# A new line of work with five-step weight decoding, queries first among the loads, and zero products behind the first scores

## The chip, the core and the metric

The kernel runs on one core of a Trainium2 chip. The core has five engines that run side by side, each through its own instructions in the order in which they stand in its queue: TensorE (PE in the profile; PEld is its weight loads), VectorE (DVE), ScalarE (ACT), GpSimd (POOL) and SyncE (SP), which here only issues loads. They meet through semaphores. The metric is the device time of one execution in microseconds (us), the median of three runs.

## The reference

Eight batches with eight heads each. 512 local queries attend to the 32 global keys and to local keys no more than 32 positions away; 32 global queries attend to all 544 keys. The result, 544 rows of 512 per batch, goes through a gated layer with a causal convolution of five taps:

```python
s_ll = np.where(np.abs(pos[:, None] - pos[None, :]) <= 32, scale * q_l @ k_l.T, -1e9)
out_l = softmax([scale * q_l @ k_g.T, s_ll]) @ [v_g, v_l]
out_g = softmax(scale * q_g @ [k_g, k_l].T) @ [v_g, v_l]
x = heads side by side of [out_g, out_l]                # (8, 544, 512)
gate = sigmoid(sum(conv_w[k] * xp[:, k:k + S] for k in range(5)))
out = (gate * (x @ w_val)) @ w_out
```

The weights and taps reach the kernel as float64 (it sees them as pairs of 32-bit words); q, k and v are float32.

## The kernel before

The work is cut into 32 units: unit u holds two heads of batch u // 4, so four units make a batch. The steps of a unit have short names, which stand in one long string, `ORDER`. That string is the order in which everything is issued; a planner outside the kernel wrote it. What follows `:` names the engine, what follows `@` the PSUM banks.

- `s` (PE, line 522): scores of a unit, 64 small products; `mx.0`, `mx.1` (DVE, 233): mask added, row minimum taken, four instructions each; `exp` (ACT, 541); `t` (PE, 555): transposes; `tc` (ACT or DVE, 331): copy out of PSUM to `pts`; `av` (PE, 574): times the values; `eps`, `norm` (DVE): division, into `xs`; `xt` (PE, 601): transposes; `xc` (ACT or DVE): copy to SBUF; `xh`, `xl`: high and low part of it for the projections.
- `gs`, `gmax`, `gexp`, `gt`, `gtc`, `gav`, `geps`, `gnorm`, `gx`, `gxc`: the same for the global queries of a batch.
- `tap`, `conv` (DVE): convolution of a unit; for the units 0 and 1 TensorE does it with diagonal matrices instead (`pc`, 678; the diagonals are `dg`, on GpSimd). `sig` (ACT): the sigmoid.
- `g1` (PE, 706) projects by w_val, `gv`, `gh`, `gl` multiply by the gate and split in high and low, `g2` (PE, 734) projects by w_out, `ob` copies the output tile, `st` stores it. Key `g` (`g1.g`, `ob.g.0`, `st.g.1`) is the same for the global rows of all batches, which come last.
- `w0` to `w7`: the decoding of eight 128x512 slices of w_val (0 to 3) and w_out (4 to 7) from float64 words to a high and a low float32 part. `w.s0` takes the magnitude (ACT or DVE), `w.s1` to `w.s7` are seven DVE instructions, `w.high` copies the high part. `cw` does the same for the taps.
- `z` (PE, 805): products of zeros, which compute nothing that is used. `zr` holds zeros as float32r, `zf` as float32.

Loads are issued by SP. The first thirteen stand in `FIRST` (w: a slice of w_val, 512 KB; m: mask and taps, 148 KB; q: queries and keys of a unit, 624 KB; v: its values, 975 KB); each later one is tied to the product before it in the line. An engine that reaches an instruction whose operand has not come waits there, and all that is queued behind it waits too.

`RINGS` gives the number of buffers for each kind of tile. The diff touches `f64_parts` (283), `taps` (312), `weight` (356), the strings, and the loop that makes the `z` steps. The last step that copies an output tile, `ob.g.1`, is split in two: ACT takes the left half, DVE the right.

## Time and profile before

| | |
|---|---|
| median of 3 runs | 350.95 us (350.72 to 354.19) |
| profiled execution, its own time | 352.35 us |
| its span | 350.6 us |
| busy: PE, DVE, ACT, POOL | 334.6, 309.0, 225.1, 13.6 us |

The span runs from the first to the last instruction; 1.75 us lie around it in the profiled execution. Busy time is the sum of the instructions of an engine. A row of the timeline gives start, length, engine, line and operation, a count where alike instructions are merged, and in brackets how long the engine had stood idle before it and which engine's work ended that.

### The profile page before, as it was taken

How to read it: one execution, taken by the hardware profiler on the slowest of the kernel's cores; microseconds unless marked ns; L12 is line 12 of the kernel's file. 1: busy time of each engine (PE TensorE's matmuls, PEld its weight loads, DVE VectorE, ACT ScalarE, POOL GpSimd, SP SyncE). 2: the span in 40 equal slices, each digit the busy share in tenths (PEclk: the TensorE clock that was granted, in tenths of full speed). 3: DMA queues.
4: the chain of work that ended last, by engine and by line, in shares of the span. 5: the costliest groups of instructions: out<-in, count | busy, mean ns of one | idle time of the engine just before them, and what ended most of it. 6: DMA issues, size and time to landing. Idle time of an engine off the chain costs nothing.

```text
span 350.6 us, 15343 instructions
## 1 busy us (share of the span) xinstructions
PE 334.6 (95%) x6658; PEld 268.9 (77%) x6658; DVE 309.0 (88%) x1035; ACT 225.1 (64%) x579; POOL 13.6 (4%) x23
## 2 busy tenths in 40 slices
PE   4889999999999989999999999999999999999994
PEld 1647678778777878887888888787888888888893
DVE  3799999999999989999999999799598898997981
ACT  2678799977878858948947459637876504434221
POOL 4013120001000000000000000000000000000000
PEclk9999999999999999999999999999999999999999
DMA  7987696798477937806393549346460200012124
GB/s 238 410 355 235 214 395 223 226 326 305 170 258 241 344 123 279 285 16 208 116 383 119 179 149 306 145 145 223 146 261 5 80 14 30 2 60 90 65 87 150
DMA packets 17107, 66.64 MB, mean 190 GB/s; under 512 B 1808, under 2 KB 3984, under 8 KB 17040
## 3 DMA queue, kind: packets, MB, share of 16 engines
q1 hardware_dynamic: 12240, 57.01, 46.1%
q10 hardware_dynamic: 4800, 8.65, 6.6%
q8 instruction: 52, 0.85, 0.9%
q14 instruction: 15, 0.12, 0.1%
HBM read 56.74 MB, written 8.91 MB: 187 GB/s over the span
## 4 chain that ended last, share of the span: by engine, by line
PE 86%; DMA 4%; DVE 4%; ACT 3%; issue 2%; ACTq 0%; SPq 0%
PE psum L706 27%; PE psum L734 25%; PE psum L522 9%; PE psum L574 8%; PE psum L263 6%; PE psum L477 3%; PE psum L601 2%; DMA v<-in_vw_dram 2%; PE psum L425 2%; DMA qk<-in_qk_dram 2%; PE psum L555 1%; DVE pm L233 1%; PE psum L678 1%; DVE wa L233 1%; ACT pm L541 1%
## 5 line engine op out<-in xcount | busy, mean ns | idle before, releaser
L233 DVE SCALAR_TENSOR_TENSOR gate<-xc,cw,gate 128x512 f32<-128x512 f32 x120 | 87.7, 751 | 1.0
L541 ACT ACTIVATE pm<-pm,mx 128x128 f32<-128x128 f32 x256 | 80.1, 394 | 10.6 <-DVE mx L233 10.6
L233 DVE CUSTOM_DVE_ANT_0 pm<-psum,small 128x128 f32<-128x128 f32 x256 | 57.8, 286 | 11.1 <-PE psum L522 11.1
L706 PE MATMUL psum<-xh,wvh 128*128 128x512 f32 x128 | 52.0, 407 | 0.0
L734 PE MATMUL psum<-woh,gh 128*128 128x512 f32 x128 | 51.7, 404 | 0.0
L706 PE MATMUL psum<-xh,wvl 128*128 128x512 f32 x128 | 50.1, 391 | 0.9 <-issue 0.9
L734 PE MATMUL psum<-wol,gh 128*128 128x512 f32 x128 | 50.0, 391 | 0.1
L734 PE MATMUL psum<-woh,gl 128*128 128x512 f32 x128 | 50.0, 391 | 0.0
L706 PE MATMUL psum<-xl,wvh 128*128 128x512 f32 x128 | 49.9, 390 | 0.0
L522 PE MATMUL psum<-qk 64*32 64x128 f32 x2048 | 37.0, 282 | 3.5 <-DMA qk<-in_qk_dram 3.3
L690 ACT ACTIVATE gate<-gate 128x512 f32<-128x512 f32 x32 | 19.8, 629 | 29.6 <-DVE gate L233 29.6
L522 PEld LDWEIGHTS psum<-qk 64*32 64x32 f32 x2048 | 30.1, 108 | 9.0 <-DMA qk<-in_qk_dram 4.9
L574 PE MATMUL psum<-v,pts 128*32 128x65 f32 x2048 | 34.4, 221 | 2.1 <-issue 1.9
L574 PEld LDWEIGHTS psum<-v,pts 128*32 128x32 f32 x2048 | 30.5, 109 | 7.4 <-issue 3.0
L331 ACT COPY pts<-psum 128x512 f32<-128x512 f32 x53 | 29.6, 586 | 5.3 <-DVE mx L233 2.8
L706 PEld LDWEIGHTS psum<-xh,wvl 128*128 128x128 f32 x128 | 24.0, 188 | 6.5 <-issue 1.3
L706 PEld LDWEIGHTS psum<-xh,wvh 128*128 128x128 f32 x128 | 24.0, 188 | 6.0 <-DVE gv L233 0.3
L734 PEld LDWEIGHTS psum<-woh,gh 128*128 128x128 f32 x128 | 24.4, 190 | 5.0 <-DVE gm L233 0.2
L734 PEld LDWEIGHTS psum<-woh,gl 128*128 128x128 f32 x128 | 24.0, 188 | 5.2
L734 PEld LDWEIGHTS psum<-wol,gh 128*128 128x128 f32 x128 | 24.1, 188 | 5.0 <-issue 0.5
L706 PEld LDWEIGHTS psum<-xl,wvh 128*128 128x128 f32 x128 | 24.1, 188 | 4.6 <-issue 0.2
L233 DVE SCALAR_TENSOR_TENSOR gv<-gate,psum 128x512 f32<-128x512 f32 x32 | 21.8, 683 | 5.9 <-PE psum L706 3.9
(124 smaller groups left out, 517.2 us busy)
## 6 DMA issues: line engine op xcount, KB each, us to landing
v<-in_vw_dram SPq DMA_DIRECT2D x32, 975.0 KB, 6.9
qk<-in_qk_dram SPq DMA_DIRECT2D x32, 624.0 KB, 5.3
out_dram<-ob ACTq DMA_DIRECT2D x32, 256.0 KB, 2.3
wraw<-in_w_val_dram SPq DMA_DIRECT2D x4, 512.0 KB, 12.5
wraw<-in_w_out_dram SPq DMA_DIRECT2D x4, 512.0 KB, 3.5
out_dram<-obg SPq DMA_DIRECT2D x4, 64.0 KB, 1.7
out_dram<-obg ACTq DMA_DIRECT2D x4, 64.0 KB, 2.0
small<-in_mask_dram SPq DMA_DIRECT2D x1, 148.0 KB, 3.3
```

The lines of the kernel that those rows point to most:

```text
L233: ins = made(*args, **kwargs)
L263: on_pe(T.matmul(out, in_, ident[D * r:D * r + D, D * r:D * r + D], is_transpose=True, **more))
L331: A.copy(out, in_)
L425: on_pe(T.matmul(s[h][SG * c:SG * c + SG, cols], qkt[rows, SL + SG * h:SL + SG * h + SG], keys, start=True, stop=True))
L477: on_pe(T.matmul(ag[SG * c:SG * c + SG, :], pgt[:k, s, SG * c:SG * c + SG], vt[:k, w, h, :], start=(n == 0), stop=(n == len(steps) - 1)))
L522: on_pe(T.matmul((sx, sy)[h][32 * j:32 * j + 32, i, :], qkt[rows, 32 * m:32 * m + 32], qkt[rows, k0:k0 + P], start=True, stop=True))
L541: A.activation(out=pm[:, h, i, :], in_=pm[:, h, i, :], func=AF.Exp, bias=mx[:, c:c + 1], scale=-1.0)
L574: on_pe(T.matmul(ax[32 * j:32 * j + 32, h, E1 * i:E1 * i + E1], q, vt[:, block_win(4 * i + j), h, :], start=True, stop=True))
L601: on_pe(T.matmul(xt[:, P * i:P * i + P], xs[:, i].rearrange("p h d -> p (h d)"), ident, start=(i == 0 or u not in XP), stop=(u not in XP), ...
L690: A.activation(out=g, in_=g, func=AF.Tanh, scale=0.5)
L706: on_pe(T.matmul(box["pv", e], w[:, e, t * P:t * P + P], x, start=(t == 0 and q == 0), stop=(t == NDT - 1 and q == 2)))
L734: on_pe(T.matmul(box["po", r], g[:, e, rs], w[:, e, :], start=(e == 0 and q == 0), stop=(e == NDT - 1 and q == 2)))
```

## The change

1. The decoding loses two of its DVE steps for each slice. Before, the low word's part was made as a float in several steps. Now the mantissa's next bits are cut out of the low word with a shift and put into the float32 word with an or (`s4`), and the low part is the difference between that float and the high part (`s5`). `w.high` now waits for `s4`, so the high part is rounded from the whole float. `cw` loses one small step.
2. `FIRST`: the first unit's queries come first, then w0 and the mask; q3 moves ahead of v0; w2 moves behind v1 and v2.
3. The line is written anew, from the first step to the last. The steps `z1.1` and `z2.0` (three float32r products of zeros) become `z2.0f` (two float32 products of zeros, behind `s0`) and one `z1.1`; `xn0` and `xn3` (a subtraction on TensorE) go, and `xl0` and `xl3` are done on DVE.
4. `RINGS`: more buffers for mx, xg, xs, ob, fewer for xc, xl, gate, xh.

```diff
-FIRST = "w0 m0 q0 q1 q2 v0 w1 w2 q3 v1 w3 v2 v3"
-RINGS = {"mx": 8, ..., "xg": 2, ..., "xc": 7, "xs": 3, ..., "xl": 6, "gate": 7, "xh": 6, "gv": 3, "ob": 6}
+FIRST = "q0 w0 m0 q1 q2 q3 v0 w1 v1 v2 w2 w3 v3"
+RINGS = {"mx": 13, ..., "xg": 5, ..., "xc": 6, "xs": 4, ..., "xl": 5, "gate": 6, "xh": 5, "gv": 3, "ob": 8}
...
-w0.s0:ACT cw dg0 w0.s1 w0.s2 s0@31 mx0.0 exp0.0 s1@50 t0.0@3 tc0.0:ACT mx0.1 mx1.0 mx1.1 exp0.1 t0.1@0 s2@43 exp1.1
+w0.s0:ACT s0@10 mx0.0 exp0.0 w0.s1 z2.0f@7 t0.0@4 mx0.1 s1@21 exp0.1 t0.1@3 tc0.0:DVE cw tc0.1:ACT gs0@35 dg0 mx1.0 s2@20
...
-    def f64_parts(raw, a, low, on=lambda n: "DVE"):
+    def f64_words(raw, a, on="DVE"):
...
-        kept = 0x3FFFFFF8 if low is None else 0x3FFFF000
...
-        power = lambda: V.tensor_scalar(out=hi, in0=a, scalar1=-0x00800000, scalar2=None, op0=ALU.bitwise_and)
-        scaled = lambda x, out: V.scalar_tensor_tensor(out=out, in0=x, scalar=2.0 ** -52, in1=hf, op0=ALU.mult,
-                                                       op1=ALU.mult)
-        if low is None:
-            return first + (power, lambda: scaled(lo.bitcast(U32), lf))
-        return first + (lambda: V.tensor_scalar(out=hi, in0=hi, scalar1=0x1FF, scalar2=None, op0=ALU.bitwise_and),
-                        lambda: V.scalar_tensor_tensor(out=lf, in0=hi, scalar=2.0 ** 32, in1=lo.bitcast(U32),
-                                                       op0=ALU.mult, op1=ALU.add),
-                        power, lambda: scaled(lf, low))
+        return (magnitude,
+                lambda: V.tensor_scalar(out=af, in0=af, scalar1=2.0 ** -15, scalar2=None, op0=ALU.max),
+                lambda: V.tensor_scalar(out=a, in0=a, scalar1=3, scalar2=0x3FFFFFF8, op0=ALU.logical_shift_left,
+                                        op1=ALU.bitwise_and),
+                lambda: V.scalar_tensor_tensor(out=a, in0=hi, scalar=-0x40000000, in1=a, op0=ALU.bitwise_and,
+                                               op1=ALU.bitwise_or),
+                lambda: V.scalar_tensor_tensor(out=a.bitcast(U32), in0=lo.bitcast(U32), scalar=29, in1=a.bitcast(U32),
+                                               op0=ALU.logical_shift_right, op1=ALU.bitwise_or))
...
+        def rest():
+            V.tensor_tensor(out=lo_t, in0=box["a"].bitcast(F32), in1=hi_t.bitcast(F32), op=ALU.subtract)
...
-        plan.add(f"w{k}.high", ("ACT", "DVE", "POOL"), high, [f"w{k}.s3"], lock=True)
+        plan.add(f"w{k}.high", ("ACT", "DVE", "POOL"), high, [f"w{k}.s4"], lock=True)
+        plan.add(f"w{k}.s5", "DVE", rest, [f"w{k}.high"], lock=True)
...
-            plan.add(name, "PE", lambda name=name: keep_clock(int(name[1:].split(".")[0]), HOME[name][0]))
+            plan.add(name, "PE", lambda name=name: keep_clock(int(name[1:].split(".")[0]), HOME[name][0], zf if name[-1] == "f" else zr))
```

The opening on SP, before (q is `qk`, w1 and w3 load into the second half of `wraw0` and `wraw2`):

```order
L349 DMA wraw0_87<-in_w_val_dram 128x4x256
L959 DMA small_71<-in_mask_dram 128x296
L349 DMA qk0_90<-in_qk_dram 128x1248
L349 DMA qk1_92<-in_qk_dram 128x1248
L349 DMA qk2_94<-in_qk_dram 128x1248
L349 DMA v0_96<-in_vw_dram 128x1950
L349 DMA wraw0_87<-in_w_val_dram 128x4x256
L349 DMA wraw2_99<-in_w_val_dram 128x4x256
L349 DMA qk3_101<-in_qk_dram 128x1248
L349 DMA v1_103<-in_vw_dram 128x1950
L349 DMA wraw2_99<-in_w_val_dram 128x4x256
L349 DMA v2_106<-in_vw_dram 128x1950
```

and now:

```order
L337 DMA qk0_87<-in_qk_dram 128x1248
L337 DMA wraw0_89<-in_w_val_dram 128x4x256
L951 DMA small_71<-in_mask_dram 128x296
L337 DMA qk1_92<-in_qk_dram 128x1248
L337 DMA qk2_94<-in_qk_dram 128x1248
L337 DMA qk3_96<-in_qk_dram 128x1248
L337 DMA v0_98<-in_vw_dram 128x1950
L337 DMA wraw0_89<-in_w_val_dram 128x4x256
L337 DMA v1_101<-in_vw_dram 128x1950
L337 DMA v2_103<-in_vw_dram 128x1950
L337 DMA wraw2_105<-in_w_val_dram 128x4x256 x2
L337 DMA v3_108<-in_vw_dram 128x1950
```

q0 comes first, q3 moves ahead of v0, and the pair w2, w3 stands behind v2 instead of around q3 and v1.

The opening on PE, before (qk0 with 32x128 is `s0`, pm0 is `t0`, v0 is `av0`, xs0 is `xt0`, qk0 with 32x384 begins `gs0`):

```order
L805 MATMUL psum_70<-zf_82 128x512 x2
L522 MATMUL psum_70<-qk0_90 32x128 x32
L522 MATMUL psum_70<-qk1_92 32x128 x32
L555 MATMUL psum_70<-ident_72,pm0_173 128x128 x8
L522 MATMUL psum_70<-qk2_94 32x128 x32
L574 MATMUL psum_70<-v0_96,pts0_175 32x65 x32
L555 MATMUL psum_70<-ident_72,pm1_216 128x128 x8
L601 MATMUL psum_70<-ident_72,xs0_335 128x128 x4
L805 MATMUL psum_70<-zr_81 128x512
L425 MATMUL psum_70<-qk0_90 32x384
```

and now:

```order
L797 MATMUL psum_70<-zf_82 128x512 x2
L514 MATMUL psum_70<-qk0_87 32x128 x32
L797 MATMUL psum_70<-zf_82 128x512 x2
L547 MATMUL psum_70<-ident_72,pm0_156 128x128 x4
L514 MATMUL psum_70<-qk1_92 32x128 x32
L547 MATMUL psum_70<-ident_72,pm0_156 128x128 x4
L417 MATMUL psum_70<-qk0_87 32x384
...
L514 MATMUL psum_70<-qk2_94 32x128 x32
L547 MATMUL psum_70<-ident_72,pm1_210 128x128 x4
L566 MATMUL psum_70<-v0_98,pts0_158 32x65 x32
L547 MATMUL psum_70<-ident_72,pm1_210 128x128 x4
L593 MATMUL psum_70<-ident_72,xs0_367 128x128 x4
```

Two float32 products of zeros stand between `s0` and `t0.0`, `s1` goes behind `t0.0`, and `gs0` moves ahead of `s2`.

ACT from `exp1.0` (before) on, around the decoding of w2 (`wa2<-wraw2`), before:

```order
L541 ACTIVATE pm1_216<-pm1_216,mx1_217 128x128 x4
L291 ACTIVATE wa1_331<-wraw0_87 128x512
L291 ACTIVATE wa2_352<-wraw2_99 128x512
L331 COPY xc0_356<-psum_70 128x512
L541 ACTIVATE pm2_276<-pm2_276,mx2_277 128x128 x4
L331 COPY pts1_218<-psum_70 128x512
L331 CAST xh0_390<-xc0_356 128x512
L331 COPY pts1_218<-psum_70 128x512
L291 ACTIVATE wa3_396<-wraw2_99 128x512
L438 ACTIVATE pg0_0_388<-pg0_0_388,gm0_0_387 128x544
L541 ACTIVATE pm2_276<-pm2_276,mx2_277 128x128 x4
L541 ACTIVATE pm3_432<-pm3_432,mx3_433 128x128 x8
```

and now, from `exp2.1` on:

```order
L533 ACTIVATE pm2_290<-pm2_290,mx2_291 128x128 x4
L288 ACTIVATE wa1_363<-wraw0_89 128x512
L430 ACTIVATE pg0_0_313<-pg0_0_313,gm0_0_312 128x544
L319 COPY pts1_212<-psum_70 128x512
L319 COPY pts2_292<-psum_70 128x512
L456 COPY pgt0_0_440<-psum_70 96x384
L457 COPY pgt0_0_440<-psum_70 128x256
L288 ACTIVATE wa2_443<-wraw2_105 128x512
L533 ACTIVATE pm2_290<-pm2_290,mx2_291 128x128 x4
L533 ACTIVATE pm3_428<-pm3_428,mx3_429 128x128 x4
L430 ACTIVATE pg0_1_446<-pg0_1_446,gm0_1_445 128x544
L533 ACTIVATE pm3_428<-pm3_428,mx3_429 128x128 x4
```

`w2.s0` still stands ahead of the first half of `exp2`, but its load now comes later, and `exp2.0`, `exp3.0`, `gexp0.1` and `exp3.1` are queued behind it.

The last rows of DVE, before (obg_1 is the right half of `ob.g.1`, ob7_2 is `ob.7.2`):

```order
L233 SCALAR_TENSOR_TENSOR gvg_2_6165<-gateg2_6001,psum_70 128x256
L233 TENSOR_TENSOR glg_6137<-gvg_2_6165,ghg_6136 128x256
L233 SCALAR_TENSOR_TENSOR gvg_3_6175<-gateg3_6004,psum_70 128x256
L233 TENSOR_TENSOR glg_6137<-gvg_3_6175,ghg_6136 128x256
L233 TENSOR_SCALAR ob7_2_6201<-psum_70 128x512
L233 TENSOR_SCALAR obg_1_6206<-psum_70 128x256
```

and now:

```order
L231 SCALAR_TENSOR_TENSOR gvg_2_6150<-gateg2_5994,psum_70 128x256
L231 SCALAR_TENSOR_TENSOR gvg_3_6152<-gateg3_5997,psum_70 128x256
L231 TENSOR_TENSOR glg_6138<-gvg_2_6150,ghg_6137 128x256
L231 TENSOR_TENSOR glg_6138<-gvg_3_6152,ghg_6137 128x256
L231 TENSOR_SCALAR obg_1_6187<-psum_70 128x256
L231 TENSOR_SCALAR obg_0_6194<-psum_70 128x512
```

The last output tile but one, `ob.g.0`, was ACT's; it is now DVE's, in one piece, behind the half of `ob.g.1`.

## Rows read from the trace of the kernel before

**Rows 1.** Page, busy us (share of the span) xinstructions of each engine.

```profile
PE 334.6 (95%) x6658; PEld 268.9 (77%) x6658; DVE 309.0 (88%) x1035; ACT 225.1 (64%) x579; POOL 13.6 (4%) x23
```

**Rows 2.** Busy time by stretch: PE, PEld, DVE, ACT, POOL (x), PEclk, DMA share, GB/s.

```profile
30.00:40.00 10.00, 9.69 (x271) 6.80 (x270) 9.91 (x35) 9.97 (x25) 4.33 (x5) 1.00 0.69 240
40.00:60.00 20.00, 19.18 (x502) 14.93 (x492) 19.32 (x83) 16.90 (x49) 1.75 (x2) 1.00 0.82 295
60.00:250.00 190.00, 187.18 (x4467) 152.65 (x4466) 178.37 (x639) 139.14 (x369) 1.74 (x2) 1.00 0.63 218
250.00:340.00 90.00, 90.00 (x947) 75.64 (x946) 77.63 (x173) 39.30 (x89) 0.00 (x0) 1.00 0.18 68
```

**Rows 3.** Instructions in order of time, PE: start, us, line, operation [idle before].

```profile
1.43 3.78 PE L805 MATMUL psum<-zf 128*128 128x512 f32 x4 [1.43 <-DVE zero L233]
8.52 3.67 PE L522 MATMUL psum<-qk 64*32 64x128 f32 x128 [3.30 <-DMA qk<-in_qk_dram]
12.12 1.00 PE L555 MATMUL psum<-ident,pm 128*128 128x128 f32 x4
15.22 1.16 PE L522 MATMUL psum<-qk 64*32 64x128 f32 x64
35.31 2.81 PE L678 MATMUL psum<-xc,diag 128*128 128x512 f32 x6
```

**Rows 4.** The same, DVE.

```profile
4.59 0.18 DVE L233 TENSOR_SCALAR cva<-small 128x20 int32<-128x20 int32 x1 [2.64 <-DMA small<-in_mask_dram]
10.58 0.29 DVE L233 CUSTOM_DVE_ANT_0 pm<-psum,small 128x128 f32<-128x128 f32 x1 [3.69 <-PE psum L522]
13.98 0.69 DVE L233 SCALAR_TENSOR_TENSOR wa<-wraw,wa 128x512 int32<-128x512 int32 x1
52.06 0.29 DVE L233 CUSTOM_DVE_ANT_0 pm<-psum,small 128x128 f32<-128x128 f32 x1
```

**Rows 5.** The same, ACT.

```profile
10.92 1.28 ACT L541 ACTIVATE pm<-pm,mx 128x128 f32<-128x128 f32 x4 [6.08 <-DVE mx L233]
```

**Rows 6.** The same, SP, which issues the loads.

```profile
11.26 0.43 SPq L349 DMA_DIRECT2D wraw<-in_w_val_dram  x1
11.74 2.06 SPq L349 DMA_DIRECT2D v<-in_vw_dram  x2
```

**Rows 7.** DMA issues of these stretches: KB each, median us from issue to landing.

```profile
wraw<-in_w_val_dram SPq DMA_DIRECT2D x1, 512.0 KB, 12.0
v<-in_vw_dram SPq DMA_DIRECT2D x1, 975.0 KB, 13.8
```

**Rows 8.** Groups of instructions, DVE: xcount | busy us, mean ns | idle before.

```profile
L233 DVE TENSOR_SCALAR wa<-wa 128x512 f32<-128x512 f32 (+1 forms) x16 | 6.9, 434 | 0.1
L233 DVE SCALAR_TENSOR_TENSOR wa<-wraw,wa 128x512 int32<-128x512 int32 x8 | 5.5, 688 | 0.1
L233 DVE SCALAR_TENSOR_TENSOR wraw<-wraw 128x512 f32<-128x512 int32 x8 | 5.6, 705 | 0.1
L233 DVE SCALAR_TENSOR_TENSOR wvl<-wraw 128x512 fp32r<-128x512 f32 x4 | 2.9, 723 | 0.0
L233 DVE TENSOR_TENSOR xl<-xc,xh 128x512 fp32r<-128x512 f32 x30 | 20.5, 685 | 0.1
L233 DVE COPY pts<-psum 128x512 f32<-128x512 f32 x11 | 7.4, 686 | 0.4 <-PE psum L263 0.4
L233 DVE CAST xh<-xc 128x512 fp32r<-128x512 f32 x9 | 3.8, 421 | 0.0
```

**Rows 9.** Instructions in order of time at the end: PE, ACT, DVE, ACT's queue.

```profile
345.64 0.39 PE L734 MATMUL psum<-woh,glg 128*128 128x512 f32 x1
346.44 0.38 ACT L740 ACTIVATE obg<-psum 128x256 f32<-128x256 f32 x1 [0.49 <-PE psum L734]
346.86 0.42 DVE L233 TENSOR_SCALAR obg<-psum 128x256 f32<-128x256 f32 x1 [4.08 <-ACT obg L740]
347.31 0.86 ACTq L946 DMA_DIRECT2D out_dram<-obg  x2
```

## The prediction

> **What bounds the kernel now.** I first read the page's busy shares: TensorE is busy for 334.6 of 350.6 us, DVE for 309.0 [rows 1]. Then the busy time by stretch: TensorE works for 187.18 of 190 us between 60 and 250, and for 90.00 of 90 from 250 to 340, while DVE and ACT still have room there. Between 30 and 60, DVE (9.91 of 10, 19.32 of 20) and, at first, ACT (9.97) are as full as TensorE [rows 2]. So behind 60 us the time is TensorE's work, which this change leaves nearly alone. What can be won is TensorE's lost time ahead of it, and there the timeline of DVE is the one to follow. Its first row minimum starts at 10.58, after 3.69 us of waiting for the first scores; these start at 8.52, after 3.30 us of waiting for a load [rows 3, 4]. From then on DVE hardly rests: 16 minimum instructions take 10.58 to 13.98, 0.85 us for a half unit, and the seventh unit's begin at 52.06 [rows 4]. I count how much earlier DVE has done the same work in the new line, and take TensorE to be as much ahead when it becomes the bound.

> **The change part by part.**

> (a) The first minimum needs the scores of unit 0 and the mask. The first zeros keep TensorE until 5.21 and the queries now come first: the 660 KB of w0 and mask, ahead of the queries before, had landed by 4.59 [rows 4], and q0 is 624 KB. The scores of two units took 3.67 us [rows 3], so `s0` ends near 7.2 with its latency. The mask now stands last of the 1,284 KB that had landed at 8.52: at the latest it comes then, at the earliest at 6.2 (4.5, and 624 KB at the rate worked out under (e)). I take 7.4: **-3.2 us** (ends -4.0 and -2.1).

> (b) Two float32 products of zeros now stand ahead of `t0.0` on TensorE. The same two took 3.78 us at the start; products of that shape take 2.81 / 3 = 0.94 each at 35 us. The scores show the same two speeds: 3.67 / 2 = 1.84 us for a unit at 8.52, 1.16 at 15.22 [rows 3]. [...] The new zeros then end between 7.2 + 1.9 = 9.1 and 7.2 + 3.8 = 11.0. `t0.0` also needs `exp0.0`, whose four activations start 0.34 us behind the first minimum and take 1.28 [rows 5]: 7.4 + 1.6 = 9.0, so the zeros decide. Its four transposes took 1.00 at 12.12 [rows 3], half of that at the higher clock. For `t0.0` waits DVE, which now does `tc0.0` ahead of the taps and of unit 1. It is there at 7.4 + 0.85 + 0.43 + 0.85 = 9.5, and the copy costs 0.69 [rows 8]. I take zeros that end at 9.9 and transposes of 0.5, a wait of 0.9: **+1.6 us**. [...]

> [...]

> (c) The decoding. Before, a slice took seven DVE steps: four on one tensor (434 ns; `s1` and `s2` have the row, and I price `s4` and `s6`, of the same shape, by it), `s3` with 688, `s5` with 705, `s7` with 685 to 723: 4 x 0.434 + 0.688 + 0.705 + 0.70 = 3.83 us. Now it takes 2 x 0.434 + 2 x 0.688 + 0.685 = 2.93, with `s5` priced as the same difference in `xl` [rows 8]. The new `s4`, a shift with an or on two tensors, has no row; its bounds are 0.434 and 0.723, and I take the 688 of `s3`, which also works on two tensors of integers. That saves 0.90 for a slice, and six slices (w0 to w5) are worked off by 52 us: **-5.4 us**.

> (d) What DVE takes over from ACT and TensorE by then: `xl0` and `xl3` (0.685 each), `xc0` out of PSUM (0.69), `xh0`, `w0.high` and `w3.s0` (0.42 each, by the row of xh), `gxc0` and `geps0` (under 0.42 together): **+3.6 us** [rows 8]. It saves ACT about as much, which is full only between 30 and 40.

> (e) w2 lands later. The loads had brought 1,284 KB at 8.5 and 6,642 KB at 11.26 + 12.0 = 23.3 [rows 3, 6, 7]: 362 KB per us. w2 now stands at 7,105 KB, so at 24.6 (v2, at 7,617 KB, had landed at 25.5). ACT's `w2.s0` follows in about 0.7, until 25.3. DVE gets to `w2.s1` at 24.0: from 7.4 on it has the minima of three units (5.1), (b), nine decoding steps (5.2), the taps (six of 0.18 as at 4.59 [rows 4]), `xc0`, `xh0`, `w0.high` (1.5), and `gmax` twice and `norm0`, priced as three copies of 0.69. That would be a wait of 1.3. But q0's 624 KB took 4.0 us behind the mask, where 1.7 would do at that rate; if this pause goes with the new order, w2 is in time. The middle: **+0.6 us** (ends 0 and the second rival).

> (f) The end. DVE now copies `ob.g.0` behind its half of `ob.g.1`, which itself waited for ACT's half: 346.44 to 346.82 on ACT, 346.86 to 347.28 on DVE. The two stores that ACT issues behind it take 0.86 us [rows 9]. Now the copy (0.69, by the row of pts [rows 8]) comes next, and two more stores stand behind those two: **+0.85 us**, at the least +0.4 if the queue takes them faster.

> Removed products: `xn0`, `xn3` and two float32r zeros go from TensorE, each under the 0.94 of a float32 product [rows 3]; the work that hides this is DVE's, which TensorE waits for at that time, so I count nothing (end -2). Gaps of TensorE between 60 and 250 are 190 - 187.18 = 2.82 us [rows 2]. The new order with its shorter rings makes its own; I take the same amount, with -1 and +2.8 as ends.

> Sum: -3.2 + 1.6 - 5.4 + 3.6 + 0.6 + 0.85 = -1.95 us. The profiled execution took 352.35, 1.4 over the median, so it would take 350.4; the median, 350.95, becomes **349.0 us**, -0.6%.

> **The rivals.** About 1% (3.5 us) is what a measurement of this kernel can tell from no change.

> *The opening works in full* (chance 0.27): mask early (-4.0), zeros short (+0.8), w2 in time (0), the rest as above: -4.15, **346.8 us**. For it: the pause of 2.3 us in the loads under (e). Against it: nothing in the rows says that the new order is rid of that pause.

> *w2 holds up ACT* (0.10), the case on the slower side. If w2 lands no sooner than v3, the last load, at 25.5 + 975 / 362 = 28.2, then ACT stands until 28.9 with four exponential steps queued behind, and DVE waits 4.9 us instead of 0.6: -1.95 + 4.3 = +2.35, **353.3 us**. The time is slower than before from a landing at 25.9 on. For it: slices of 512 KB land late here, 12.0 us behind their issue. Against it: v3 is issued behind w2.

> *The opening's gain is spent in the middle* (0.13): xc, xl, xh and gate each lose a buffer, and TensorE's gaps of 2.82 us double: **351.8 us**. For it: every step stands in a new place. Against it: the old line, written in the same way, left only 2.82 us in 190.

> *The zeros do not do what they are there for* (0.08): the clock stays at 1.2 GHz, (b) is +3.2: **350.6 us**.

> **The numbers.** The forecast has 0.42, and is the likeliest. Its own ends are 347.5 and 350.3. Taking in the first rival, the unknown gaps on its side, and the second rival, 8 times in 10 the time lies between 346.0 and 352.4. Faster by over 1% (under 347.4) is the first rival and a sliver of the forecast: 0.28. Slower by over 1% (over 354.5) needs two of the slower cases together: 0.06. The rest, 0.66, is within 1%.

> **What would show it.** Right: the scores start at about 5.2, the first minimum at 7.2 to 8.5; DVE waits for TensorE ahead of `tc0.0` for up to 1 us and for `w2.s0` near 25; the seventh unit's minimum starts between 45 and 48, with `conv3.0` and the second batch's `gmax` still to come; a slice has five DVE steps of 2.9 us; and 4.5 + 0.85 us lie between the last product and the end. Wrong: a first minimum at 8.5 or later (mask), zeros that end at 11 (b), a wait of DVE or ACT for w2 of more than 2 us (e), over 4 us of gaps in TensorE from 60 to 250, or an end no longer than before (f).

## The result

| | before | changed |
|---|---|---|
| median, first set of runs | 351.88 us | 353.45 us |
| ratio to the kernel before, 95% interval | | 1.0065 (1.0040 to 1.0089) |
| the same kernel once more, another set (`e12_again`) | 352.33 us | 353.25 us, 1.0030 (1.0000 to 1.0061) |
| profiled execution: time, span | 352.35, 350.6 us | 354.58, 352.8 us |
| start of TensorE's last product | 345.64 us | 347.03 us |
| from that product's end to the span's end | 4.57 us | 5.38 us |

The forecast was 349.0 us with a range up to 352.4. By the two sets the change makes the kernel 0.65% and 0.3% slower, the latter with an interval that begins at no change at all: still within the 1% that I called no change, but on the other side, and outside the range. The ratios and their intervals come from the single runs; they need not equal the quotient of the two medians (1.0045 and 1.0026).

### The profile page after: what moved, and what is told of

It is laid out like the page before. It is cut to its first block, busy times and chain, and to the rows that moved or that the text cites. A ratio compares the mean times of both kernels' runs of the same rounds, so it can differ in the third digit from the quotient of the medians.

```text
span 352.8 us, 15328 instructions
## 1 busy us (share of the span) xinstructions
PE 335.9 (95%) x6663; PEld 268.5 (76%) x6663; DVE 309.0 (88%) x1024; ACT 222.7 (63%) x573; POOL 12.9 (4%) x23
## 4 chain that ended last, share of the span: by engine, by line
PE 87%; DVE 3%; DMA 2%; issue 2%; ACT 2%; POOL 1%; DVEq 0%; ACTq 0%
PE psum L726 27%; PE psum L698 25%; PE psum L514 8%; PE psum L566 8%; PE psum L261 6%; PE psum L417 2%; PE psum L469 2%; DMA v<-in_vw_dram 2%; PE psum L670 2%; PE psum L593 2%; PE psum L797 2%; PE psum L547 1%; POOL diag L231 1%; DVE wa L231 1%; ACT pm L533 1%
## 5 line engine op out<-in xcount | busy, mean ns | idle before, releaser
L319 ACT COPY pts<-psum 128x512 f32<-128x512 f32 x49 | 27.8, 587 | 14.1 <-PE psum L261 8.6
L514 PEld LDWEIGHTS psum<-qk 64*32 64x32 f32 x2048 | 29.3, 105 | 7.6 <-issue 4.1
```

The source lines that it names most:

```text
L319: A.copy(out, in_)
L514: on_pe(T.matmul((sx, sy)[h][32 * j:32 * j + 32, i, :], qkt[rows, 32 * m:32 * m + 32], qkt[rows, k0:k0 + P], start=True, stop=True))
```

## The profile after

The page's line of busy time [rows 1] hardly moves: DVE is at 309.0 again, since what the decoding saves goes into copies and splits that ACT or TensorE did before.

```profile
PE 335.9 (95%) x6663; PEld 268.5 (76%) x6663; DVE 309.0 (88%) x1024; ACT 222.7 (63%) x573; POOL 12.9 (4%) x23
```

Busy time by stretch, in the columns of [rows 2], with the first 30 us in front:

```profile
0.00:17.00 17.00, 13.13 (x308) 7.68 (x308) 9.63 (x60) 7.29 (x19) 4.83 (x13) 1.00 0.91 349
17.00:30.00 13.00, 12.03 (x180) 6.56 (x168) 11.74 (x44) 10.48 (x30) 1.18 (x2) 1.00 0.92 335
30.00:40.00 10.00, 7.92 (x238) 5.46 (x239) 8.84 (x34) 7.29 (x19) 4.10 (x5) 1.00 0.67 212
40.00:60.00 20.00, 18.44 (x418) 13.65 (x420) 18.44 (x79) 15.80 (x42) 1.23 (x2) 1.00 0.77 266
60.00:250.00 190.00, 187.00 (x4556) 153.37 (x4557) 175.80 (x630) 137.26 (x366) 1.53 (x2) 1.00 0.63 214
250.00:340.00 90.00, 90.00 (x950) 75.61 (x949) 81.29 (x175) 42.01 (x95) 0.00 (x0) 1.00 0.19 71
```

The kernel before, same stretches:

```profile
0.00:17.00 17.00, 10.94 (x232) 6.93 (x236) 8.88 (x52) 7.28 (x19) 4.75 (x13) 1.00 0.88 321
17.00:30.00 13.00, 11.60 (x246) 7.26 (x235) 12.65 (x54) 10.14 (x28) 1.01 (x1) 1.00 0.80 308
```

Add TensorE's busy time up to 60 us: 13.13 + 12.03 + 7.92 + 18.44 = 51.52 us, of which 1.98 are the new zeros. Before it was 10.94 + 11.60 + 9.69 + 19.18 = 51.41. **In this execution TensorE has, by 60 us, where it becomes the bound, done no more work than before.** It wins in the first 30 us and gives it back between 30 and 60. Busy time is a rough count of work (before, the first two units' scores took 3.67 us of it, now 2.32), and this execution is the latest of six that share this opening: it reaches record 2,500 of TensorE's stream (counted as below) at 62.27 us, the five others (`e12_again`, `e2_idle_load`, `e3_tail`, `e5_late_load`, `e15_two_loads`) at 59.97 to 61.08, with 52.7 to 53.6 us of busy time by 60. Of the kernel before there is one profiled execution.

TensorE in order of time (answers to [rows 3]; last column: idle before, and what ended it):

```profile
5.03 1.16 PE L514 MATMUL psum<-qk 64*32 64x128 f32 x64
6.12 1.98 PE L797 MATMUL psum<-zf 128*128 128x512 f32 x4
8.82 1.16 PE L514 MATMUL psum<-qk 64*32 64x128 f32 x64
12.44 0.86 PE L514 MATMUL psum<-qk 64*32 64x128 f32 x41
15.05 0.51 PE L514 MATMUL psum<-qk 64*32 64x128 f32 x17 [1.76 <-issue]
37.23 0.33 PE L491 MATMUL psum<-ident,xg 128*128 128x128 f32 x1 [1.57 <-DVE xg L231]
57.88 0.50 PE L698 MATMUL psum<-xl,wvh 128*128 128x512 f32 x1 [1.33 <-issue]
117.12 0.76 PE L469 MATMUL psum<-v,pgt 96*32 96x65 f32 x34 [1.39 <-DMA v<-in_vw_dram]
165.76 0.34 PE L261 MATMUL psum<-ident,pm 64*128 64x64 f32 x4 [0.46 <-issue]
190.13 0.32 PE L566 MATMUL psum<-v,pts 128*32 128x65 f32 x8 [0.79 <-issue]
```

DVE (answers to [rows 4]):

```profile
6.89 0.29 DVE L231 CUSTOM_DVE_ANT_0 pm<-psum,small 128x128 f32<-128x128 f32 x1 [4.95 <-DMA small<-in_mask_dram]
8.93 0.69 DVE L231 COPY pts<-psum 128x512 f32<-128x512 f32 x1
15.61 0.29 DVE L231 CUSTOM_DVE_ANT_0 pm<-psum,small 128x128 f32<-128x128 f32 x1 [1.30 <-PE psum L514]
34.13 0.69 DVE L231 TENSOR_TENSOR wvl<-wa,wvh 128x512 fp32r<-128x512 f32 x1 [1.06 <-POOL wvh L231]
47.82 0.32 DVE L231 CUSTOM_DVE_ANT_0 pm<-psum,small 128x128 f32<-128x128 f32 x1
```

The opening starts better than forecast: first minimum at 6.89 (before 10.58), no wait ahead of `tc0.0` at 8.93, seventh unit's minimum at 47.82 (before 52.06). But TensorE stops for 1.76 us in the midst of `s2`, between two products with the same operands at hand, and DVE's next minimum, unit 2's, waits 1.30 us for it. The "issue" idle is the profile's word for a wait for nothing that it shows. The second loss is at 34.13: DVE's `w1.s5` needs `w1.high`, which POOL does behind five diagonals (`dg1`), and behind DVE stands `gnorm0`, for which TensorE waits until 37.23.

What "issue" is can be counted out. I numbered TensorE's records in the trace (weight loads, products, and the 50 of its sequencer) from the first on, and put beside them when the DMA queue that the page calls "instruction" started a packet. It has 52 packets of 16 KB. The stream has 13,376 records, with 52 borders if one stands every 256 records from 193 on (the last is 13,249).

```profile
q8 instruction: 52, 0.85, 1.0%
```

```
                number of the record behind the stall; (its rest modulo 256); stall, us
before          1473 (193) 0.82   3009 (193) 0.88   5825 (193) 1.03
changed          449 (193) 1.76   2241 (193) 1.33   7873 (193) 0.46   8897 (193) 0.79
changed, again   449 (193) 1.36   2241 (193) 0.52   4033 (193) 0.36   4801 (193) 1.25   5825 (193) 0.63   8897 (193) 0.51
```

Every one stands at the border of a block of 256 records, and the packet for that block started 2.3 to 2.9 us before TensorE went on (12.62 for 15.05, 55.56 for 57.88). So TensorE's instructions come by DMA, a block at a time, and TensorE stalls where it is through with one before the next has come. That loads on the DMA engines hold the blocks up is what the experiments test.

## Experiments

All are timed against the kernel before; the changed kernel stands at 1.0065 and 1.0030. The stalls (TensorE's "issue" idle of over 0.15 us) are those of the one profiled execution.

**Where the borders fall.** `keep_clock` cuts the two opening products of zeros into pieces, so that everything behind stands later in the stream:

```diff
-        for _ in range(n):
-            on_pe(T.matmul(psum[:, b, :], z[:, :P], z, start=True, stop=True))
+        for c in range(0, n * SL, w):
+            on_pe(T.matmul(psum[:, b, c % SL:c % SL + w], z[:, :P], z[:, c % SL:c % SL + w], start=True, stop=True))
...
-    keep_clock(2, 7, zf)
+    keep_clock(2, 7, zf, 32)
```

> The changed kernel with the two opening products of zeros cut into 32 pieces of 32 columns: the same columns on TensorE, but 128 instructions in place of 8, so that everything behind them stands 120 instructions later in TensorE's stream. Theory A (the 'issue' idle is the instruction stream: blocks of 256 instructions are fetched by DMA, and a border that comes before its block has landed stalls): no stall of 1.76 us between the 41st and 42nd product of s2; every 'issue' stall of over 0.3 us stands again at an instruction number that is 193 modulo 256, so at other products than before, and at each of them the block's 16 KB landed 1.2 to 1.5 us earlier. The time moves with the sum of the new stalls (they sum to 5.7 us in the changed kernel): anything from -2 to +3 us. Theory B (these idle times belong to the plan: a buffer or a DMA that the products wait for): the stall stays inside s2, at the same product, within 0.3 us of 1.76, and the time within 0.5 us of the changed kernel's, ratio to the kernel before 1.005 to 1.008.

Measured: 406.44 us, ratio 1.150 (1.143 to 1.158). That is far outside what either theory allowed, since the edit was too coarse: the 64 instructions of 32 columns took 13.86 us in place of 3.67, so some 10 us are a late start. Of the rest, 31.5 us are 16 "issue" stalls, all at 193 modulo 256, the longest 4.07 us; what is left over goes with a lower granted clock, 0.960 on average against 0.996. So with 128 columns a piece (`..., 128)`), 24 instructions more, for 3.78 us of zeros in both kernels (3.67 and 3.78 without), on the changed kernel and on the one before:

> The changed kernel with the two opening products of zeros cut into 8 pieces of 128 columns: 32 instructions in place of 8, for about the same time on TensorE (in 32 pieces of 32 columns each instruction pair took 0.217 us, in pieces of 512 columns 0.92, so 128 columns should take 0.22 to 0.26 and all sixteen 3.5 to 4.2 us against 3.67). Everything behind stands 24 instructions later. Theory A (block borders): the stalls stand at 193 modulo 256 again, 24 instructions earlier in the program than in the changed kernel; the time moves with them, by -2 to +10 us (the shift by 120 raised the sum of the gaps to over 30 us). Theory B: the borders don't matter, and the 50 us of the shift by 120 came from its late start: here the start is the same, the time within 1 us of the changed kernel's, ratio to the kernel before 1.003 to 1.009.

> The kernel before with its two opening products of zeros cut into 8 pieces of 128 columns, the same 24 instructions more that cost the changed kernel 9 us. Nothing else differs from the kernel before. Theory A (where a line's borders fall is a property of the line, and the kernel before stands as well as it does only in its own place): stalls at 193 modulo 256 again, their sum 3 to 12 us in place of 2.7, time +2 to +10 us, ratio 1.006 to 1.03. Theory B (only the changed line packs its short products so closely that a border can stall it): sum of the stalls within 1.5 us of 2.7, time within 1.5 us, ratio 0.996 to 1.004.

Measured: changed + 24: 362.60 us, **1.0270** (1.0203 to 1.0337), eleven stalls, 11.6 us in all. Before + 24: 362.46 us, **1.0287** (1.0245 to 1.0330), ten, 11.2 us. TensorE, before + 24:

```profile
42.04 0.89 PE L574 MATMUL psum<-v,pts 128*32 128x65 f32 x48 [1.12 <-issue]
63.11 0.39 PE L706 MATMUL psum<-xh,wvl 128*128 128x512 f32 x1 [0.50 <-issue]
70.23 2.02 PE L574 MATMUL psum<-v,pts 128*32 128x65 f32 x128 [3.16 <-issue]
```

The same work in the same order costs 10 us more when its borders stand 24 instructions elsewhere. About 1.0 us of this is not at a border: before + 24, a unit of scores took 1.96 us at 15.35 in place of 1.16, and TensorE was 1.0 us late where the kernel before has its record 600. Theory A holds, and for the old line too. Both lines stand where they do only at their own places; no run here shows a shift that leaves either of them faster.

**What the block waits for.** In a stretch without loads, four loads that nothing reads, issued ahead of a border; the same four 8 us later; two of them at the first place:

```diff
-... g1.5.3.0@0 g1.5.3.1 ...
+... g1.5.3.0@0 ix0 ix1 ix2 ix3 g1.5.3.1 ...
+    for i in range(4):
+        plan.add(f"ix{i}", "SP", lambda i=i: transfer(sb.tile([P, QK], F32, tag="qk", name=f"idle{i}", bufs=RINGS["qk"]), qk[i]))
```

> The changed kernel with four loads of 624 KB that nothing reads, issued behind the first product of g1.5.3 (about 273.7 us), where the DMA engines are idle but for a store. The loads take about 6 us of the DMA engines, from about 275.7 to 282. Theory A (instruction blocks queue behind loads): the block that now starts at 278.7 and lands at 280.0 starts 1 to 3 us later, and TensorE stalls 1 to 3 us at instruction 12737 (now crossed at 281.25 with no gap), an 'issue' idle in the midst of the out products; no other engine or wait changes before that; the time rises by the stall, ratio to the kernel before 1.010 to 1.015. Theory B (loads that nothing reads can't hold TensorE): no stall there, the time as the changed kernel's, ratio 1.005 to 1.008.

> The control of the idle loads: the same four loads of 624 KB that nothing reads, put 9 us later in the line, behind the product g2.5.0.3 (about 282.6 us), when the block for instruction 12737 has long landed and the next border (12993) is 26 us away. Theory A (only a block fetched while loads fill the DMA engines stalls TensorE): no stall at 12737 over 0.3 us and none at 12993; the time as the changed kernel's, ratio to the kernel before 1.003 to 1.009, against 1.0195 with the loads at 271.7. Rival (loads cost by their bytes, wherever they stand): the same +4.4 us as with the early loads.

> The idle loads once more at their first place, behind the first product of g1.5.3, two in place of four (1.25 MB). Four held the block up until their bytes were through (it started 5.14 us behind the border, and TensorE stalled 3.51 us). If the block waits for what is queued ahead of it: two are through about 3.3 us earlier, the block starts 1.0 to 2.5 us behind the border, the stall is 0 to 1.0 us, and the time within 1 us of the changed kernel's, ratio 1.003 to 1.010. If any load in flight costs the block the same: the stall is 3 us or more again, ratio 1.015 to 1.02.

Measured: four early 357.88 us, 1.0195 (1.0154 to 1.0237), more than either theory had; four late 352.66 us, 1.0031 (0.9997 to 1.0065); two early 353.83 us, 1.0055 (1.0027 to 1.0083). Four early, TensorE and SP's queue:

```profile
278.95 0.40 PE L726 MATMUL psum<-woh,gh 128*128 128x512 f32 x1
282.86 0.79 PE L726 MATMUL psum<-wol,gh 128*128 128x512 f32 x1 [3.52 <-issue]
283.45 0.63 PE L726 MATMUL psum<-woh,gl 128*128 128x512 f32 x1
```

```profile
271.73 2.73 SPq L337 DMA_DIRECT2D idle<-in_qk_dram  x4
```

Two early, at the same product:

```profile
280.15 0.51 PE L726 MATMUL psum<-wol,gh 128*128 128x512 f32 x1 [0.49 <-issue]
```

The border before (12481) was crossed at 275.48; the block for 12737 started at 280.51, 5.0 us later, where it is 0.9 us in the changed kernel. With two loads it is 2.1 us. The late four cost nothing, though the DMA engines were as full (share 0.99 from 282 to 286). So it is loads queued when a block is wanted that cost. The stall costs more than its length, too: from 282 to 286 the granted clock was 0.57, and products followed each other by 0.43 us in place of 0.23.

**Half the packet.** Loads of q, k and v from unit 4 on in two halves (on the kernel with the two repairs below):

```diff
-        transfer(t, qk[u])
+        for c in ([slice(0, QK)] if u < 4 else [slice(0, QK // 2), slice(QK // 2, QK)]):
+            transfer(t[:, c], qk[u][:, c])
...
```

> The kernel with both repairs, and every load of q, k and v from unit 4 on in two transfers of half the columns each: the same bytes, packets of half the size. If a block waits for the packet that its DMA engine is moving, the delay from a border to the start of the fetch under full load (2 to 5 us) falls by about half, and the sum of the stalls behind 60 us (0.8 to 3.4) by 0.5 to 2 us: ratio 0.990 to 0.996. If it waits for the bytes queued ahead of it, the delays stay, and smaller packets move less per us: ratio 0.997 to 1.006.

Measured: 352.05 us, 0.9996 (0.9974 to 1.0019), against 0.9976 without the halves; seven stalls of 4.7 us in all. Smaller packets do not help. A packet of the loads' queue took 0.13 us on average in place of 0.21, and where loads filled the wait (a DMA share of over 0.85), a block still started 2.6 us behind the border before it, against 2.5 without the halves (means of 20 and 17 blocks). With the two loads in place of four this speaks for the queue ahead, not for the packet in flight. One packet of 0.21 us gives no reason for a wait of 5.0 us. Why the block comes so late is open.

**The zeros**, and **the five-step decode alone** (the old line, first loads and rings):

```diff
-... w0.s1 z2.0f@7 t0.0@4 ...
+... w0.s1 t0.0@4 ...
```

> The changed kernel without its second pair of zeros (z2.0f; TensorE then has nothing between s0, which ends at 6.2, and t0.0, which starts at 7.9). If the zeros hold TensorE's clock up: t0.0, s1 and what follows run at half rate, s1 in 1.9 to 2.0 us in place of 1.16, and TensorE is 1 to 3 us later at 13 us; time +0.5 to +2 us, ratio to the kernel before 1.006 to 1.012. If they do nothing here: t0.0 and s1 as before (0.95, 1.16 us), VectorE's first 16 us the same; the instructions behind stand 8 earlier in the stream, and the time moves by the stalls alone, -1.5 to +1.5 us.

Measured: 355.90 us, 1.0110 (1.0061 to 1.0160). TensorE's opening without them:

```profile
4.86 1.16 PE L514 MATMUL psum<-qk 64*32 64x128 f32 x64
7.52 1.11 PE L547 MATMUL psum<-ident,pm 128*128 128x128 f32 x4 [1.50 <-ACT pm L533]
8.56 1.16 PE L514 MATMUL psum<-qk 64*32 64x128 f32 x64
```

`s1` takes 1.16 us either way. At the same place of the program (record 2,500) TensorE is at 60.28, with the zeros at 60.41 (`e3_tail`). Its last product then comes 4.65 us later than there, and its stalls are 3.8 us more (5.5, one of 2.17 us at 191 us, against 1.7); behind that one the granted clock was 0.66 from 191 to 196. The zeros did nothing for the clock of the opening in these executions. Whether they count as eight instructions, by other borders, is not shown: the interval of this time reaches down into the changed kernel's (to 1.0089), and the four stalls stand at records that stalled in that kernel too.

```diff
-... w2.s4 wi4 w2.s5 ... w2.s6 w4.s1 w2.s7 ... w2.high:ACT ...
+... w2.s4 wi4 ... w4.s1 w2.high:ACT w2.s5 ...
```

> The kernel before with the five-step decode alone (its own line, first loads and rings; each slice's old steps 5 and 6 gone, its old step 7 replaced by the subtraction; w2.high moved ahead of that subtraction, w7.high behind step 4). My step (c): VectorE does 0.90 us less for each of 6 slices ahead of 54 us, 5.4 us in all, plus the later two. Theory A (VectorE sets the end of the opening there): mx6.0 comes 3 to 5 us earlier than 52.06, time -3 to -5 us, ratio 0.986 to 0.992. Theory B (TensorE and its instruction stream set it, VectorE only in part): VectorE's idle grows by about what its work falls, mx6.0 1 to 2.5 us earlier, time -2.5 to 0 us, ratio 0.993 to 1.000; 'issue' stalls at 193 modulo 256 again, at the same numbers as before (the stream has the same instructions in the same places) but of other lengths.

Measured: 352.86 us, 1.0015 (0.9982 to 1.0049). This is theory B's time. By the busy time of the stretches, DVE works 38.02 us from 17 to 60 in place of 41.88, and in its place stand waits that the kernel before had not (the line numbers are this kernel's):

```profile
26.33 0.29 DVE L132 CUSTOM_DVE_ANT_0 pm<-psum,small 128x128 f32<-128x128 f32 x1 [1.14 <-PE psum L415]
32.35 0.69 DVE L132 TENSOR_TENSOR wvl<-wa,wvh 128x512 fp32r<-128x512 f32 x1 [0.56 <-ACT wvh L220]
40.18 0.20 DVE L132 RECIPROCAL mx<-mx 128x8 f32<-128x8 f32 x1 [1.09 <-ACT mx L226]
47.80 0.69 DVE L132 TENSOR_TENSOR xl<-xc,xh 128x512 fp32r<-128x512 f32 x1 [0.45 <-ACT xh L220]
```

Between the first and the seventh unit's minimum, before and here (columns as in [rows 2]):

```profile
10.58:52.06 41.48, 37.62 (x940) 26.09 (x927) 39.88 (x167) 34.83 (x92) 7.09 (x8) 1.00 0.85 316
9.81:51.19 41.38, 37.28 (x914) 25.64 (x918) 35.39 (x155) 35.11 (x93) 6.14 (x8) 0.97 0.84 302
```

DVE works 4.5 us less and stands idle 4.4 us more (41.38 - 35.39 = 5.99 in place of 1.60). Its seventh minimum comes 0.87 us earlier, less than theory B's 1 to 2.5, and the first one already came 0.77 earlier. TensorE, with the same stream in both, reaches record 2,241 at 56.32 (before 56.84), and its last product 0.4 us earlier: of 4.5 us of DVE's time, half a microsecond arrives.

**Repairs.** The tail in order, and `w1.high` on ACT where it is idle:

```diff
-... g2.g.0.3 ob.7.1:ACT st.5.3 g2.g.1.0@4 ... ob.7.0:ACT st.6.2 st.7.1 st.7.0 ob.g.1 st.g.1 ob.g.0:DVE st.g.0
+... g2.g.0.3 ob.7.1:ACT st.5.3 ob.7.0:ACT st.6.2 st.7.1 ob.g.0:DVE st.7.0 st.g.0 g2.g.1.0@4 ... ob.g.1 st.g.1
```

```diff
-... w2.s3 exp2.0 av1@5 ... w3.s1 w1.high:POOL norm1 ...
+... w2.s3 exp2.0 w1.high:ACT av1@5 ... w3.s1 norm1 ...
```

> The changed kernel with the global rows' last two evictions put back in order: ob.7.0 and its stores, then ob.g.0 (on VectorE) and st.g.0, ahead of the last four products g2.g.1, and ob.g.1 and st.g.1 alone behind them. My step (f): the half of ob.g.1 on VectorE no longer has ob.g.0 beside it and four stores in place of eight stand behind the last product: span's end 0.8 us nearer to the last product (now 5.3 us behind it, then 4.5), time -0.8 us, ratio to the kernel before 1.003 to 1.005. Rival: the end is set by the last store's own flight and not by their number: -0.3 us or less, ratio 1.005 to 1.008.

> The changed kernel with w1.high on ScalarE behind exp2.0 (ScalarE is idle for 1.98 us there, 24.3 to 26.3) in place of POOL behind five diagonal products (done at 34.1): VectorE no longer waits 1.06 us at w1.s5 for wvh. Theory A: that wait is the one between the early start and a shorter time; gnorm0 and TensorE's xg transpose come 1.0 us earlier, TensorE's 1.57 us of idle before it falls to 0.3 to 0.7, time -1.0 us, ratio to the kernel before 1.003 to 1.005. Theory B (what is won ahead of a block border of the instruction stream is lost at it, or by a stall at another): the wait goes, TensorE is ahead at 38 us by about 1 us, and the sum of 'issue' stalls behind it changes by as much or more; time between -2 and +1.5 us, not tied to the 1 us won.

> The changed kernel with both repairs: the tail's evictions in order (alone 1.000 to the kernel before) and w1.high on ScalarE (alone 1.0035). If the two add up: -2.0 and -1.0 us to the changed kernel's 1.0065, ratio 0.997 to 0.999. If the 1 us won at w1.high is lost again at the border at 104 us (0.96 us stall at instruction 4801 with it, none or 0.6 without): ratio 0.999 to 1.002, as with the tail alone; TensorE 1 us earlier up to 90 us and not behind 110.

Measured: tail 351.37 us, 1.0000 (0.9972 to 1.0029), better than the 1.003 to 1.005 that I expected; `w1.high` 353.53 us, 1.0035 (1.0000 to 1.0071); both 351.06 us, 0.9976 (0.9943 to 1.0008). The end of the kernel with the tail in order, PE, ACT, DVE and ACT's queue:

```profile
344.28 0.39 PE L726 MATMUL psum<-woh,glg 128*128 128x512 f32 x1
...
344.70 0.38 ACT L732 ACTIVATE obg<-psum 128x256 f32<-128x256 f32 x1 [3.62 <-DMA out_dram<-obg]
345.12 0.42 DVE L231 TENSOR_SCALAR obg<-psum 128x256 f32<-128x256 f32 x1 [2.44 <-ACT obg L732]
345.58 0.85 ACTq L938 DMA_DIRECT2D out_dram<-obg  x2
```

and of the changed kernel (answers to [rows 9]):

```profile
347.03 0.39 PE L726 MATMUL psum<-woh,glg 128*128 128x512 f32 x1
347.46 0.38 ACT L732 ACTIVATE obg<-psum 128x256 f32<-128x256 f32 x1 [3.62 <-PE psum L726]
347.87 1.02 DVE L231 TENSOR_SCALAR obg<-psum 128x256 f32<-128x256 f32 x2 [4.56 <-ACT obg L732]
348.33 1.81 ACTq L938 DMA_DIRECT2D out_dram<-obg  x4
```

From the last product's end to the span's end it is 4.13 us with the repair, 5.38 without: 1.25 us. By the ratios the repair gains 2.3 us on the changed kernel's first set and 1.1 on the second, so the end is between half and all of it. What there is beyond may be stalls (1.7 us in this profiled execution, 4.3 and 4.8 in the two of the changed kernel); one trace does not show it for a median. Of `w1.high`, theory B holds as far as one execution shows. Its wait goes, and TensorE's wait for xg is 0.59 us in place of 1.57:

```profile
35.62 0.33 PE L491 MATMUL psum<-ident,xg 128*128 128x128 f32 x1 [0.59 <-DVE xg L231]
104.02 0.43 PE L514 MATMUL psum<-qk 64*32 64x128 f32 x10 [0.96 <-issue]
```

At record 2,500 TensorE is 1.23 us ahead of the kernel with the tail alone (59.18 against 60.41), at 4,289 still 0.75 (92.53, 93.28), and at 5,000 no more (108.43, 108.38): between them stands the border at 104.02. In `e10_both`, with `w1.high` moved too, TensorE is at record 2,500 only at 60.53: its stall in `s2` was 1.72 us, and the granted clock was 0.59 from 16 to 20. With both repairs the time was 0.24% below the kernel before, which the interval does not settle.

**The border inside s2.** With both repairs, `s1` ahead of `t0.0`, so that record 193 comes earlier; the zeros once cut to 64 columns behind `s1`, once left whole ahead of it:

```diff
-... z2.0f@7 t0.0@4 mx0.1 s1@21 exp0.1 ...
+... s1@21 z2.0f@7 t0.0@4 mx0.1 exp0.1 ...
...
-            on_pe(T.matmul(psum[:, b, :], z[:, :P], z, start=True, stop=True))
+            on_pe(T.matmul(psum[:, b, :w], z[:, :P], z[:, :w], start=True, stop=True))
```

```diff
-... z2.0f@7 t0.0@4 mx0.1 s1@21 exp0.1 ...
+... z2.0f@7 s1@21 t0.0@4 mx0.1 exp0.1 ...
```

> The kernel with both repairs, and the third border made earlier: s1 stands directly behind s0 (its q1 lands at about 7.2 us by the bytes moved), and z2.0f, cut to 64 columns, behind it, so that the stream keeps its length and every later border its place. Without the zeros nothing was lost in the first 60 us but their 8 instructions' place, so they are not needed for the clock. Theory A: instruction 193 is crossed at 7.4 to 8.2 us in place of 9.0, its block's successor is fetched 0.8 to 1.5 us earlier, and the stall inside s2 (1.0 to 1.8 us in every execution so far) falls to 0 to 0.6 us; TensorE is 0.8 to 1.3 us earlier at instruction 600; of that 0 to 1.3 us reach the end. Ratio 0.994 to 1.002. Theory B (the stall in s2 has another cause): it keeps its length, and the time is that of the kernel with both repairs.

> The kernel with both repairs, and s1 ahead of t0.0 with the zeros left whole between s0 and s1 (TensorE then has no pause of 2.15 us before s1, which in the run with s1 directly behind s0 was followed by products at half rate up to 16 us). s1 starts at 8.1 to 8.3 in place of 8.8. Theory A: instruction 193 is crossed 0.6 to 0.8 us earlier, the block for 449 comes as much earlier, and the stall inside s2, 1.0 to 1.8 us in every execution of the changed line, falls to 0.2 to 1.1; t0.0 and what hangs on it is 1.1 us later, so that at instruction 600 TensorE is 0 to 0.5 us ahead, or behind. Ratio 0.994 to 1.002. Theory B: the stall keeps its 1.0 to 1.8 us.

Measured: `e11` 351.62 us, 0.9971 (0.9934 to 1.0009); its profiled execution took 358.28, so I read nothing from its trace. `e13` 350.44 us, 0.9980 (0.9950 to 1.0011), TensorE:

```profile
14.19 0.51 PE L514 MATMUL psum<-qk 64*32 64x128 f32 x17 [0.32 <-issue]
```

The stall inside `s2`, 1.00 to 1.76 us in every other execution that kept the line's order there, is 0.32: theory A. Against `e10_both`, 0.6 us are left at record 600 (16.39, 17.00), and none at record 2,500 (60.58, 60.53): `e13_s1_zeros` stalls 1.51 us at 2,241, `e10_both` 0.52.

> The changed kernel itself once more, beside the others on the same chip. If the block fetches make the spread between executions: the opening up to 14 us the same within 0.3 us, and the sum of the stalls other than the 4.3 us of the first profile (here 1.5 to 5), its time following that sum; the stall inside s2 present again (1.0 to 1.8), the 1.33 us one at instruction 2241 possibly not. Rival: the stalls are fixed by the program: the same four, each within 0.3 us. Ratio to the kernel before 1.004 to 1.009 by either.

Measured: as in the first table. Six stalls of over 0.3 us, 4.6 us in all, two of the four of the first profile missing or under half their length, three new ones. The opening agreed within 0.3 us up to 14. The program sets where a stall can be; the execution, how long it is.

## Why the prediction was wrong

**The step that failed** is the one that joined the parts: "I count how much earlier DVE has done the same work in the new line, and take TensorE to be as much ahead when it becomes the bound". The parts (a) to (e) add up to 2.8 us. DVE was not 2.8 us ahead on the same work, and TensorE did not get what DVE had.

DVE, up to the first and from there to the seventh unit's minimum, before (the second stretch stands under `e6_five_alone`) and now, and the second half of `gmax1`, before and now:

```profile
0.00:10.58 10.58, 5.85 (x84) 3.22 (x92) 3.09 (x12) 2.15 (x3) 4.75 (x13) 1.00 0.77 269
0.00:6.89 6.89, 5.46 (x70) 2.54 (x71) 1.03 (x3) 2.02 (x3) 1.54 (x8) 1.00 0.74 246
6.89:47.82 40.93, 35.22 (x872) 22.63 (x878) 36.76 (x162) 28.82 (x78) 9.18 (x12) 1.00 0.85 311
```

```profile
51.42 0.72 DVE L233 CUSTOM_DVE_ANT_0 pg<-psum,zero 128x544 f32<-128x544 f32 x1
51.69 0.72 DVE L231 CUSTOM_DVE_ANT_0 pg<-psum,zero 128x544 f32<-128x544 f32 x1
```

- **(a) held as a start and failed as a term.** The first minimum came 3.7 us earlier (forecast 3.2), the scores at 5.03. But the kernel before used its wait for the scores: DVE did the taps and two steps of w0 in it, 3.09 us of work ahead of the first minimum against 1.03 now. These 2.1 us now stand behind the first minimum. I counted them on the way to `w2.s1` in (e) and gave them no term in the sum.
- **(b) was too large.** DVE did not wait for `t0.0`: 0 in place of 0.9, so the part was the 0.7 us of the copy in place of +1.6. TensorE had the higher of its two speeds from `s0` on (1.16 us for a unit, 1.98 for the two zeros), where I had left open which it would have. Without the zeros the scores were as quick (1.16 us, `e8_no_zeros`), so these executions do not show that the zeros had a part in it. No run shows the +0.8 and +3.2 that two rivals take for (b), nor the 1.2 GHz that one of them names: the part was +0.7, the zeros behind `s0` took 1.98 us where +3.2 needs 3.8, and the traces give the clock as a share, not in GHz.
- **(c), (d) held on DVE.** The new `s4` took 0.69, as priced, and the seventh unit's minimum came at 47.82, in the window of 45 to 48 that I had named. That is 4.2 us earlier, but not on the same work: `conv3.0` and `gmax1`, some 2.4 us of DVE, stood ahead of it before and now stand behind, and the second half of `gmax1` starts at 51.69, before at 51.42. On the same work DVE is at most 1.8 us ahead, not 2.8.
- **(e) named a wait that hardly came, and others came.** DVE did not wait for w2; ACT waited 0.54 us at 22.45. But between the two minima DVE stood idle for 40.93 - 36.76 = 4.17 us, before for 41.48 - 39.88 = 1.60: 1.30 for the stalled `s2`, 0.68 for ACT's `w1.s0`, 0.31 for `av1`, 1.06 for `w1.high`. In the five other executions of this opening it was 3.5 to 4.0. I had 0.9 and 0.6, both elsewhere.
- **(f) held**: +0.81 us between last product and end, forecast +0.85.
- **From DVE to TensorE.** An engine that is busy ahead of the bound is not yet the bound: `e6_five_alone` shows 4.5 us of DVE's work gone and 0.5 us arriving. In its own profiled execution the changed kernel's TensorE had no lead at all at 60 us.
- **"Gaps of TensorE: I take the same amount"** failed with it. Take each last product's start less its stalls, an estimate that counts every stall in full: 345.64 - 2.73 = 342.9 before; for the changed line 342.7 (first profile), 342.0 (again), 342.6 (`e3_tail`) and 341.3 (`e5_late_load`). Without stalls the change wins 0.2 to 1.6 us, not 2.8. The stalls, 4.3 and 4.8 us in the first two and 1.7 and 2.2 in the others against 2.7 in the one execution of the kernel before, take this back and more in two of the four. I had the 16 KB packets in the page and did not ask what they were.

None of the five signs of being wrong came, and the time was outside the range all the same: they look at the mask, the zeros, w2, TensorE behind 60 us and the end, none at what DVE waits for between 10 and 50 us.

Of the rivals, none named it. *w2 holds up ACT* has the nearest time (353.3) and a cause that did not happen: ACT waited 0.54 us for w2 and went on at 22.45, not at 28.9. *The opening's gain is spent in the middle* (351.8) put it down to gaps behind 60 us, which stayed as they were (3.00 us against 2.82). *The zeros do not do what they are there for* was right that the zeros did nothing for the clock (`s1` took 1.16 us with them and without) and wrong that it stays low.

The account: the medians differ by 353.45 - 351.88 = 1.6 us (0.9 in the second set), the spans of the profiled executions by 2.2: +0.8 for the end, which stays in every execution, and +1.4 for the last product, the latter +1.6 of stalls (4.33 against 2.73) and -0.2 of all the rest. How the medians split between stalls and the rest is open: only single executions were profiled.

## What to carry to other kernels

Where an engine is to become the bound later, count its own work done up to that point, not the lead of the engine that feeds it; and when a wait is shortened, ask what work was done in it. On TensorE with many short products, number the instructions: a new order also moves the borders of its blocks, and 24 instructions more can cost more than the change under test is worth (1.0270 against 1.0065 here). Four loads that queued ahead of a border behind a run of short products cost time (`e2_idle_load`, 1.0195 against 1.0065); moving the kernel's own away was not tried. Shift both kernels before you believe a difference of 1%.
